# Weight preparation regrouped, three staging buffers in rotation and mixtures issued earlier, in a fused attention and two-layer MoE kernel

## The chip, the cores and the metric

The kernel runs on one core of a Trainium2 chip. The metric is the device time of one execution in microseconds, and a smaller number is better. The engines are named as the profile names them: PE (matrix multiply; PEld is its weight load), DVE (vector), ACT (scalar and activation functions), POOL (general purpose) and SP (here only the issuer of DMAs).

## The reference

```python
attn = softmax_causal(q @ k.T / 8) @ v        # 2 batches, 12 heads, 448 tokens, head size 64
x = attn as (896 tokens, 768)
h = x @ moe_w_in                              # 768 x 2048
g = where(h >= 1, h, where(h <= -1, 0, (h + 1)**2 / 4))
x = g @ moe_w_out                             # 2048 x 768
xn = x / sqrt(mean(x*x) + 1e-6) * rms_g
out = (silu(xn @ w_gate) * (xn @ w_val)) @ w_out2   # 768 x 1536 twice, 1536 x 768
```

The weights arrive as 64-bit floats.

## The kernel before

**Precision and weights.** Each operand of a matmul is split into a high and a low part in the PE's fp32r format, and a product is three matmuls per block of the contraction: high by high, high by low, low by high. A block of weights of 128 x 768 (an item) goes through steps that `w_run` issues one at a time between the matmuls, at a rate set by `w_pace` and `RATE` (four times the number is the steps per call), no further than `w_cap`; `w_need` issues whatever is still missing. A plain item has four steps (`plain_steps`): `w_low` (ACT scales the upper word, line 167, and POOL makes the lower bits from a byte, line 175), `w_sign` (empty for all but the first items), `w_high` (DVE joins both into an fp32 value, line 193) and `w_lo` (`parts`: ACT rounds the value to the high part, line 200, and POOL subtracts it, line 201). The items are loaded by DMAs of 768 KB into three staging buffers; the next load into a buffer is issued by `w_next` when its item has been used.

**Order of the work.** Attention first; then the two token halves go through w_in (line 370) and w_out (line 632, `out1`, half 0, then half 1); then the gate and value products (line 728, `product`, 9 matmuls of 448 columns each); then w_out2 (line 884, `out2`, half 0, then half 1). Every engine works off its queue in the order in which this Python issues the instructions.

**Second product.** Gate and value are computed by a scheme of seven products per block f of 128 hidden columns and both halves (Strassen with common sums), on sums of weights (`pair_steps`, blocks of 5 or 7 parts) and on mixtures T1 to T4 and B22 of the two normalised halves (`mix_a`, `mix_b`, made in PSUM and SBUF after `rms_sum` and `rms_spread` of half 1). The first NA = 4 blocks get two of the seven as `head(f)` and `tail(f)` from plain gate items, while the mixtures are made. A block's gate and value items were put through 1 + 6 steps into `rawg`, `rawv` and `sraw`; `sraw` lies in the third staging buffer, so that gate, value and all later items use two, and w_out2's items three. Block 0 is prepared during `out1`, block 1 between the mixtures and in iteration 0, each later one during the iteration before its own. The result of each product is taken over at once by DVE or ACT (`p1` to `p7`), and the weight steps come after that.

```python
for p, g, n in run:
    if g >= 0:
        p(g)                       # product and its take-over
    w_run(n if f < NF - 1 else 2)
```

**Last product.** `out2(0)` prepares one w_out2 item for each group of 18 matmuls (`w_pace(1)`, four steps) and splits one activation (`split2`, lines 867 and 868).

Of the kernel before, what the change touches and what calls it, by code (L numbers as in the profile page):

```python
# [16 lines left out]
ALU = mybir.AluOpType  # L17
# [24 lines left out]
def kernel(  # L42
# [387 lines left out]
    rawv = AF.at(TMO, NK * P)  # L430
    sraw = AF.at(STO + 2 * 2 * NK * P, 4, KP)

# [8 lines left out]
    def pair_steps(n, f):  # L441
        bl = block(f)
        g1, g2 = rawg[:, :KP], rawg[:, KP:]
        v1, s1, s2 = (bank(i)[:, :KP] for i in (5, 6, 7)) if f else (rawv[:, :KP], sraw[:, 2], sraw[:, 3])
        v2, s3, s4 = rawv[:, KP:], sraw[:, 0], sraw[:, 1]
        s12 = pst[:, 6:8, :KP] if f else sraw[:, 2:4]

        def tt(out, a, b, op):
            nc.vector.tensor_tensor(out=out, in0=a, in1=b, op=op)  # L449

        def gate_low():
            w_low(n)
# [12 lines left out]
        def sums_a():
            tt(s1, v1, v2, ALU.add)
            tt(s3, g1, v1, ALU.subtract)

        def sums_b():
            tt(s2, s1, g1, ALU.subtract)  # L470
            tt(s4, g2, s2, ALU.subtract)
            parts(bl[:, 0, 4], bl[:, 1, 4], v2)

        def parts_a():
            nc.scalar.copy(bl[:, 0, 0:2], s12)
            tt(bl[:, 1, 0:2], s12, b32(bl[:, 0, 0:2]), ALU.subtract)

        def parts_b():
            parts(bl[:, 0, 2:4], bl[:, 1, 2:4], sraw[:, 0:2])
            if f == NF - 1:  # L480
                w_load(n + 2)

        return [gate_low], [gate_high, val_high, sums_a, sums_b, parts_a, parts_b]

# [4 lines left out]

    def plain(src, dst, st, early):  # L490
        work.append(plain_steps(len(items)))
        items.append((src, dst, early, st))

    def pair(f):
        work.extend(pair_steps(len(items), f))
        items.append((w_gate[f], None, False, len(items) % 2))
        items.append((w_val[f], None, False, len(items) % 2))

    assert len(items) % 2 == 0 and NA % 2 == 0
    for f in range(NA):  # L500
        plain(w_gate[f], gslot(f), len(items) % 2, False)
    for f in range(NF):
        pair(f)
    W2_FIRST = len(items)
    for kk in range(NF):
        plain(w_out2[kk * P:(kk + 1) * P], AR.at(W2_AT[kk], 2, NK * P), (2, 0, 1)[kk % 3], kk > 0)
    for w in work:
        steps.extend(w)
        ends.append(len(steps))

    body = tc.manual_schedule()
# [69 lines left out]
    if True:  # L581
# [7 lines left out]
        def gsplit(h, kk):  # L589
            t = gj[ngj[0] % 2] if ngj[0] not in (NM - 2, NM - 1) else AR.at(XO + (ngj[0] % 2) * 2 * S, 2, S)  # L590
# [35 lines left out]
        def out1(h, after, finish):  # L626
# [34 lines left out]

        def squares(h):
            def f(dm, y):
                sq, acc = SQ[h][dm % 2], ACC[h]
                nc.scalar.activation(sq if dm else acc, y, ACTF.Square)
                nc.scalar.activation(XF[h][dm], y, ACTF.Copy, scale=gvec[:, dm:dm + 1])
                if dm and h == 0:
                    nc.gpsimd.tensor_tensor(out=acc, in0=acc, in1=sq, op=ALU.add)
                elif dm:
                    nc.vector.tensor_tensor(out=ysum if dm < NK - 1 else acc, in0=ysum if dm > 1 else acc, in1=sq,  # L670
                                            op=ALU.add)
            return f
# [79 lines left out]

        XA = [bank(i % 2)[:, :S] for i in range(HK)]
        XB = [bank(2 + i % 2)[:, :S] for i in range(HK)]
        t2 = ysum

        def sub(out, a, b):
            nc.vector.tensor_tensor(out=out, in0=a, in1=b, op=ALU.subtract)

        def mix_a(i):  # L760
            x0 = XF[0]
            normalise(1, i, XA[i])
            normalise(1, i + HK, XB[i])
            xt = XF[1][i]
            sub(xt, XA[i], x0[i])
            sub(t2, XB[i], xt)
            operand(T1, i, xt)
            operand(T2, i, t2, nc.vector)

        def mix_b(i):  # L770
            x0 = XF[0]
            sub(x0[i], t2, x0[i])
            sub(x0[i + HK], x0[i + HK], t2)
            operand(T3, i, x0[i])
            operand(B22, i, XB[i], nc.vector)
            operand(T4, i, x0[i + HK])

        w_need(2 * NM + NA + 2)
        w_cap[0] += 2
# [12 lines left out]
        mix_b(1)  # L792
        tail(2)
        w_run(1)
        mix_a(2)
        tail(3)
        mix_b(2)

        yb = [bank(f % 2) for f in range(NF)]
        zb = [bank(2 + f % 2) for f in range(NF)]  # L800
        cb = bank(4)

        def p1(f):
            product(yb[f], op(f, A11), B11)
            nc.scalar.copy(A[f][1], yb[f][:, :S])

        def p6(f):
            product(yb[f], op(f, S2), T2, first=f < NA)
            if f < NA:
                add(TMP[f][0], yb[f], A[f][1])  # L810
# [3 lines left out]
        def p7(f):  # L814
            product(zb[f], op(f, S3), T3)

        def p5(f):
            product(yb[f], op(f, S1), T1, first=False)
            if f < NA:
                add(TMP[f][1], yb[f], A[f][1])  # L820
                nc.scalar.activation(A[f][0], A[f][0], ACTF.Silu)
            else:
                nc.scalar.copy(TMP[f][1], yb[f][:, :S])
            add(TMP[f][1], zb[f], TMP[f][1])

        def p2(f):
            product(cb, op(f, A12), B21)
            add(A[f][0], cb, A[f][1])
            nc.scalar.activation(A[f][0], A[f][0], ACTF.Silu)

        def p4(f):
            z = zb[f][:, :S]
            product(zb[f], op(f, A22), T4, first=False)
            add(z, zb[f], TMP[f][0])
            mul(A[f][0], z, A[f][0])

        def p3(f):
            y = yb[f][:, :S]
            product(yb[f], op(f, S4), B22, first=False)
# [3 lines left out]
            mul(A[f][1], y, TMP[f][1])  # L843

        NP2 = 2 * NM + NA
        for f in range(NF):
            w_need(NP2 + 2 * f + 2)
            w_cap[0] = NP2 + 2 * f + 4 if f < NF - 1 else W2_FIRST + 4
            if f < NA:
                m = f < 2  # L850
                run = [(p4, f - 1, 2), (p6, f, 2), (p7, f, 1), (p5, f, int(m)), (p3, f - 1, 2 - m)]
            else:
                run = [(p1, f, 1), (p4, f - 1, 1), (p6, f, 1), (p3, f - 1, 1), (p7, f, 1), (p5, f, 1), (p2, f, 1)]
# [96 lines left out]
```

## Time and profile before

| what | us |
|---|---|
| runs of the kernel | 638.01, 639.08, 640.96 |
| median | 639.08 |
| profiled execution | 638.73 |
| its span, first to last instruction | 637.0 |
| PE busy in it | 592.3 (93%) |
| DVE, ACT, POOL busy | 320.8, 331.2, 273.9 |
| mean granted PE clock | 0.981 |

The profile is of one execution. Its own time is 1.73 us more than its span. PE is the busiest engine by far; what can be gained is PE's idle time and the time in which its clock was below full.

### The profile page before, as it was taken

The numbers are of one execution on the slowest core, as the hardware profiler recorded it, in microseconds if no ns is written. First come the engines' busy times: TensorE is split into PE (matmuls) and PEld (weight loads), VectorE is DVE, ScalarE is ACT, GpSimd is POOL, SyncE is SP. The second block draws the span as 40 slices with busy tenths as digits, with TensorE's granted clock in tenths as the row PEclk, the third lists the DMA queues.
The fourth block names the chain that finished last, engine by engine and source line by source line (L and its number), as shares of the span: only waits on it lengthen the run. The fifth ranks groups of instructions, "written<-read, shape, count | busy, mean of one in ns | idle before, by whom it ended". The sixth has DMA issues, their size and how long they took to land.

```text
span 637.0 us, 8655 instructions
## 1 busy us (share of the span) xinstructions
PE 592.3 (93%) x3236; PEld 510.5 (80%) x3236; DVE 320.8 (50%) x592; ACT 331.2 (52%) x648; POOL 273.9 (43%) x222
## 2 busy tenths in 40 slices
PE   6999999999999999999988888699999976979997
PEld 4666667999999899999977677599888865768997
DVE  5877871343233333412456877657677625553210
ACT  5888884466675734453435644355544535443212
POOL 3445432455655445441451643636655435661000
PEclk9999999999999999999999989899999978999999
DMA  8334311045444343210241124223333324421102
GB/s 292 98 128 138 118 50 50 7 158 182 151 155 170 120 149 109 90 50 6 94 145 55 50 82 166 100 99 100 118 133 140 106 100 148 150 99 46 42 1 86
DMA packets 17274, 68.19 MB, mean 107 GB/s; under 512 B 2064, under 2 KB 6672, under 8 KB 17232
## 3 DMA queue, kind: packets, MB, share of 16 engines
q1 hardware_dynamic: 17232, 67.64, 31.7%
q8 instruction: 25, 0.41, 0.3%
q14 instruction: 17, 0.14, 0.1%
HBM read 64.88 MB, written 2.75 MB: 106 GB/s over the span
## 4 chain that ended last, share of the span: by engine, by line
PE 61%; POOL 12%; DVE 11%; issue 10%; ACT 4%; DMA 2%; POOLq 0%; SPq 0%; ACTq 0%; DVEq 0%
PE ps L370 18%; PE ps L632 14%; PE ps L884 9%; POOL ar L201 6%; PE ps L276 5%; POOL af L175 5%; PE ps L728 5%; PE ps L307 4%; PE ps L355 4%; DVE af L193 3%; DVE af L449 2%; PE ps L341 2%; DVE ps L449 1%; DMA af<-in_w_out 1%; ACT ar L702 1%
## 5 line engine op out<-in xcount | busy, mean ns | idle before, releaser
L201 POOL TENSOR_TENSOR ar<-af,ar 128x768 fp32r<-128x768 f32 (+1 forms) x80 | 142.0, 1775 | 216.6 <-ACT ar L200 211.7
L728 PE MATMUL ps<-ar 128*128 128x448 f32 x756 | 167.8, 382 | 21.0 <-DVE af L738 5.3
L728 PEld LDWEIGHTS ps<-ar 128*128 128x128 f32 x756 | 146.8, 197 | 41.2 <-DVE af L738 7.8
L632 PE MATMUL ps<-ar 128*128 128x448 f32 x576 | 118.3, 366 | 2.4 <-ACT ar L592 2.0
L193 DVE SCALAR_TENSOR_TENSOR af<-af 128x768 int32<-128x768 int32 (+1 forms) x73 | 78.0, 1070 | 81.9 <-POOL af L175 81.7
L370 PE MATMUL ps<-ar 128*128 128x448 f32 x576 | 117.5, 366 | 0.0
L632 PEld LDWEIGHTS ps<-ar 128*128 128x128 f32 x576 | 107.9, 188 | 12.0 <-ACT ar L592 2.4
L370 PEld LDWEIGHTS ps<-ar 128*128 128x128 f32 x576 | 108.0, 188 | 8.6
L200 ACT CAST ar<-af 128x768 fp32r<-128x768 f32 (+1 forms) x80 | 65.6, 819 | 81.8 <-DVE af L193 81.7
L884 PE MATMUL ps<-ar 128*128 128x448 f32 x432 | 89.9, 368 | 10.0 <-DVE ar L868 8.4
L884 PEld LDWEIGHTS ps<-ar 128*128 128x128 f32 x432 | 80.5, 188 | 19.5 <-DVE ar L868 11.2
L175 POOL TENSOR_SCALAR af<-af 128x768 int32<-128x768 uint8 x72 | 73.4, 1019 | 14.4 <-DMA af<-in_w_out 5.1
L167 ACT ACTIVATE af<-af 128x768 f32<-128x768 f32 x66 | 58.6, 905 | 35.4 <-DMA af<-in_w_out 22.9
L593 DVE TENSOR_TENSOR ar<-af,ar 128x448 fp32r<-128x448 f32 x32 | 27.5, 864 | 67.4 <-ACT ar L592 67.4
L291 ACT ACTIVATE af<-ps,nm 112x336 f32<-112x336 f32 (+2 forms) x96 | 46.9, 501 | 7.6 <-DVE nm L283 7.6
L868 DVE TENSOR_TENSOR ar<-af,ar 128x448 fp32r<-128x448 f32 x24 | 27.0, 1140 | 45.9 <-ACT ar L867 45.9
L283 DVE CUSTOM_DVE_ANT_0 ps<-ps,af 112x336 f32<-112x336 f32 (+2 forms) x96 | 41.5, 474 | 13.0 <-PE ps L276 11.9
L276 PE MATMUL ps<-af 64*112 64x448 f32 (+3 forms) x192 | 35.5, 451 | 5.4 <-DVE af L254 5.3
L592 ACT CAST ar<-af 128x448 fp32r<-128x448 f32 x32 | 17.8, 565 | 34.9 <-PE ps L632 34.8
L383 DVE SCALAR_TENSOR_TENSOR af<-af,ps 128x448 f32<-128x448 f32 x32 | 19.3, 616 | 26.1 <-ACT af L379 26.1
L378 ACT ACTIVATE af<-ps,half 128x448 f32<-128x448 f32 x32 | 20.1, 629 | 20.8 <-PE ps L370 20.8
L307 PE MATMUL ps<-ident,af 112*112 112x112 f32 x240 | 30.6, 266 | 0.0
(79 smaller groups left out, 481.0 us busy)
## 6 DMA issues: line engine op xcount, KB each, us to landing
af<-in_w_out SPq DMA_DIRECT2D x28, 768.0 KB, 4.2
af<-in_w_in SPq DMA_DIRECT2D x16, 768.0 KB, 4.3
af<-in_w_gate SPq DMA_DIRECT2D x16, 768.0 KB, 4.3
af<-in_w_val SPq DMA_DIRECT2D x12, 768.0 KB, 4.3
af<-in_kT SPq DMA_DIRECT2D x12, 224.0 KB, 2.6
af<-in_qT SPq DMA_DIRECT2D x12, 224.0 KB, 3.5
af<-in_v SPq DMA_DIRECT2D x12, 224.0 KB, 2.5
out_T<-af SPq DMA_DIRECT2D x12, 224.0 KB, 1.9
```

Source lines behind the costliest of these rows:

```text
L167: nc.scalar.activation(c, c, ACTF.Prelu, scale=2.0 ** -112, alpha=-2.0 ** 32)
L175: nc.gpsimd.tensor_scalar(out=words(n, 0, I32), in0=b, scalar1=1.0 / 32, scalar2=-31.0 / 64, op0=ALU.mult, op1=ALU.add)
L193: nc.vector.scalar_tensor_tensor(out=out.bitcast(I32), in0=words(n, 1, I32)[:, c], scalar=3, in1=words(n, 0, I32)[:, c], op0=ALU.logical_s ...
L200: nc.scalar.copy(hi, src)
L201: nc.gpsimd.tensor_tensor(out=lo, in0=src, in1=b32(hi), op=ALU.subtract)
L276: nc.tensor.matmul(bs[j][:C, o:o + (c + 1) * C], lhsT=q[r, c * C:(c + 1) * C], rhs=k[r, :(c + 1) * C], start=True, stop=True, skip_group_c ...
L291: nc.scalar.activation(Pn[:C, j, poff[c]:poff[c] + w], sbank[n][j][:C, o:o + w], ACTF.Exp, bias=nm[:C, j, c:c + 1], scale=-1.0, accum_out= ...
L307: nc.tensor.transpose(bs[j][:C, o:o + C], Pn[:C, j, poff[c] + kc * C:poff[c] + (kc + 1) * C], ident[:C, :C])
L370: nc.tensor.matmul(out, lhsT=w[:, a, k * P:(k + 1) * P], rhs=x[:, c, k], start=(k == 0 and n == 0), stop=(k == NK - 1 and n == 2))
L632: nc.tensor.matmul(ybs[dm][:, :S], lhsT=w[:, a, dm * P:(dm + 1) * P], rhs=t[:, c], start=(n == 0 and i == 0), stop=(n == NM - 1 and i == 2))
L728: nc.tensor.matmul(b[:, :S], lhsT=w(a, k), rhs=x[:, c, k], start=first and k == 0 and i == 0, stop=(k == HK - 1 and i == 2), skip_group_ch ...
L884: nc.tensor.matmul(obs[dm][:, :S], lhsT=w[:, a, dm * P:(dm + 1) * P], rhs=t[:, c], start=(kk == 0 and i == 0), stop=(kk == NF - 1 and i == 2))
```

## The change

Weight steps are regrouped so that the instructions of one step do not wait for one another on another engine; the steps of a pair are six (`low`, `high`, `sums_a`, `sums_b`, `hi`, `lo`), both items together. The working space `sraw` leaves the staging buffer, and all items rotate over three. Blocks 0 and 1 of the second product are both prepared during `out1` of half 1, in SBUF (`pre`), and `RATE[5]` is 0.6 in place of 0.42; four more buffers serve the last splits there. In the loop over blocks, weight steps are issued between a product and its take-over. The mixtures keep three sets of PSUM banks, and the low halves of T1 and T2 and all of T4 and B22 are made later; `head(1)` moves ahead of `rms_sum(1)`; the last three scalings of half 1 are issued after its last square; a Silu on a small tile is issued after the Sqrt. `p3` of the block before moves ahead of `p7` in the first blocks. w_out2's items go through three steps (`low`, `high` into `rawg` or `rawv`, `parts`), those of three successive items interleaved, and `out2(0)` issues three steps per group.

```diff
-    RATE = (0.35, 0.35, 0.8, 0.2, 0.6, 0.42)
+    RATE = (0.35, 0.35, 0.8, 0.2, 0.6, 0.6)
...
     def pair_steps(n, f):
+        pre = f < 2
+        sr = AF.at(3 * S, 4, KP) if pre else AF.at((2 * NM - 4) * S, 2, KP)
+        v1, s1, s2 = (rawv[:, :KP], sr[:, 2], sr[:, 3]) if pre else (bank(i)[:, :KP] for i in (5, 6, 7))
...
-        return [gate_low], [gate_high, val_high, sums_a, sums_b, parts_a, parts_b]
+        def low():
+            w_low(n)
+            w_low(n + 1)
+        def high():
+            w_high(n, rawg)
+            w_next(n)
+            w_high(n + 1, v1, v2)
+            w_next(n + 1)
+        def sums_a():
+            if f >= NA:
+                parts(bl[:, 0, 5:7], bl[:, 1, 5:7], rawg.rearrange("p (a b) -> p a b", a=2))
+            parts(bl[:, 0, 4], bl[:, 1, 4], v2)
             tt(s1, v1, v2, ALU.add)
             tt(s3, g1, v1, ALU.subtract)
         def sums_b():
             tt(s2, s1, g1, ALU.subtract)
             tt(s4, g2, s2, ALU.subtract)
+        def hi():
+            nc.scalar.copy(bl[:, 0, 0:2], s12)
+            nc.scalar.copy(bl[:, 0, 2:4], sr[:, 0:2])
+        def lo():
             tt(bl[:, 1, 0:2], s12, b32(bl[:, 0, 0:2]), ALU.subtract)
+            nc.gpsimd.tensor_tensor(out=bl[:, 1, 2:4], in0=sr[:, 0:2], in1=b32(bl[:, 0, 2:4]), op=ALU.subtract)
+        return [], [low, high, sums_a, sums_b, hi, lo]
...
+    def w2_steps(n):
+        raw = (rawg, rawv)[n % 2]
+        dst = items[n][1]
+        def high():
+            w_high(n, raw)
+            w_next(n)
+        return [lambda: w_low(n), high, lambda: parts(dst[:, 0, :], dst[:, 1, :], raw)]
...
+    for i in range(NF + 2):
+        for j in range(3):
+            if 0 <= i - j < NF:
+                steps.append(w2[i - j][j])
...
+            elif ngj[0] > NM + 10:
+                t = AR.at(XO + 2 * NK * S + SLOT + (ngj[0] % 4) * 2 * S, 2, S)
...
-                    w_cap[0] = 2 * NM + min(NA + 2, max(0, n - 2))
+                    w_cap[0] = 2 * NM + min(NA + (2 if n < 12 else 4), max(0, n - 2))
...
             nc.scalar.activation(r, ms, ACTF.Sqrt)
+            if h:
+                nc.scalar.activation(t, ms, ACTF.Silu)
...
+        M1 = [bank(i)[:, :S] for i in (0, 1, 5)]
+        M2 = [bank(i)[:, :S] for i in (2, 3, 2)]
+        def mix(i):
+            x0, xb = XF[0][i], XF[1][i + HK]
+            normalise(1, i, M1[i])
+            normalise(1, i + HK)
+            sub(M1[i], M1[i], x0)
+            sub(M2[i], xb, M1[i])
+            sub(x0, M2[i], x0)
+            hi(T2, i, M2[i])
+            operand(T3, i, x0)
+            hi(T1, i, M1[i])
+        def mix_late(i):
+            x0 = XF[0][i + HK]
+            sub(x0, x0, M2[i])
+            operand(T4, i, x0)
+            operand(B22, i, XF[1][i + HK])
-        w_need(2 * NM + NA + 2)
+        w_need(2 * NM + NA + 4)
         head(0)
+        head(1)
         r1 = rms_sum(1)
-        head(1)
+        tail(0)
         rms_spread(1, r1)
-        mix_a(0)
-        tail(0)
-        mix_b(0)
+        mix(0)
         tail(1)
-        w_run(1)
         head(2)
-        mix_a(1)
+        mix(1)
         head(3)
-        mix_b(1)
+        lo(T2, 0, M2[0])
+        mix_late(0)
         tail(2)
-        w_run(1)
-        mix_a(2)
+        mix(2)
         tail(3)
-        mix_b(2)
+        lo(T2, 1, M2[1])
+        lo(T2, 2, M2[2])
-        yb = [bank(f % 2) for f in range(NF)]
-        zb = [bank(2 + f % 2) for f in range(NF)]
+        yb = [bank(f % 2 if f else 4) for f in range(NF)]
+        zb = [bank(2 + f % 2 if f else 6) for f in range(NF)]
...
             if f < NA:
-                m = f < 2
-                run = [(p4, f - 1, 2), (p6, f, 2), (p7, f, 1), (p5, f, int(m)), (p3, f - 1, 2 - m)]
+                run = [(4, f - 1, 1), (6, f, 1), (3, f - 1, 2), (7, f, 1), (5, f, 1)]
...
             for p, g, n in run:
                 if g >= 0:
-                    p(g)
+                    PRODUCT[p][0](g)
                 w_run(n if f < NF - 1 else 2)
+                if g >= 0:
+                    PRODUCT[p][1](g)
+                if f == 0 and p == 6:
+                    for i in range(HK):
+                        lo(T1, i, M1[i])
+                    mix_late(1)
+                    mix_late(2)
...
         p4(NF - 1)
-        w_run(2)
+        p4_post(NF - 1)
         split2(2)
         p3(NF - 1)
-        w_run(2)
+        p3_post(NF - 1)
...
-                    w_cap[0] = len(items)
-                    w_pace(1)
+                    w_run(3)
```

## Rows read from the trace of the kernel before

**Rows 1.** The page's span in 40 equal slices: PE's busy tenths and its granted clock.
```profile
PE   6999999999999999999988888699999976979997
...
PEclk9999999999999999999999989899999978999999
```

**Rows 2.** Groups by line, PE: busy us, mean ns, idle before and its releasers.
```profile
L728 PE MATMUL ps<-ar 128*128 128x448 f32 x756 | 167.8, 382 | 21.0 <-DVE af L738 5.3 <-DVE af L741 4.6 <-ACT af L812 4.0
...
L632 PE MATMUL ps<-ar 128*128 128x448 f32 x576 | 118.3, 366 | 2.4 <-ACT ar L592 2.0 <-DVE ar L593 0.2 <-DVE af L383 0.2
...
L884 PE MATMUL ps<-ar 128*128 128x448 f32 x432 | 89.9, 368 | 10.0 <-DVE ar L868 8.4 <-ACT ar L867 1.6
```

**Rows 3.** Timeline of PE, 312 to 640 us: start, us, instructions, idle before.
```profile
334.23 0.47 PE L632 MATMUL ps<-ar 128*128 128x448 f32 x1 [2.04 <-ACT ar L592]
334.89 6.75 PE L632 MATMUL ps<-ar 128*128 128x448 f32 x32 [0.19 <-DVE ar L593]
...
363.19 3.01 PE L728 MATMUL ps<-ar 128*128 128x448 f32 x9 [2.29 <-DVE af L758]
...
374.92 11.28 PE L728 MATMUL ps<-ar 128*128 128x448 f32 x54 [1.69 <-DVE af L738]
...
410.81 44.75 PE L728 MATMUL ps<-ar 128*128 128x448 f32 x207 [4.09 <-DVE af L741]
...
496.86 13.03 PE L728 MATMUL ps<-ar 128*128 128x448 f32 x63 [0.56 <-ACT af L805]
...
520.19 6.15 PE L728 MATMUL ps<-ar 128*128 128x448 f32 x18 [4.03 <-ACT af L812]
528.08 5.51 PE L728 MATMUL ps<-ar 128*128 128x448 f32 x18 [1.74 <-DVE af L738]
...
573.67 3.91 PE L884 MATMUL ps<-ar 128*128 128x448 f32 x18 [1.17 <-DVE ar L868]
578.76 54.79 PE L884 MATMUL ps<-ar 128*128 128x448 f32 x269 [1.17 <-DVE ar L868]
```

**Rows 4.** Windows: stretch, its length, busy of PE, PEld, DVE, ACT, POOL, then PEclk.
```profile
411.00:425.00 14.00, 14.00 (x59) 12.78 (x60) 7.16 (x13) 5.54 (x10) 6.46 (x5) 0.83 0.32 108
...
512.00:540.00 28.00, 19.13 (x72) 16.15 (x71) 11.21 (x13) 12.14 (x18) 12.11 (x9) 0.82 0.40 140
```

**Rows 5.** Timeline, all engines, 545 to 570 us, in out2(0).
```profile
566.19 1.86 POOL L201 TENSOR_TENSOR ar<-af,ar 128x768 fp32r<-128x768 f32 x1 [2.01 <-ACT ar L200]
566.61 1.93 DVE L868 TENSOR_TENSOR ar<-af,ar 128x448 fp32r<-128x448 f32 x1 [1.43 <-ACT ar L867]
...
569.32 0.96 DVE L193 SCALAR_TENSOR_TENSOR af<-af 128x768 int32<-128x768 int32 x1 [0.78 <-POOL af L175]
```

**Rows 6.** Groups by line, the other engines.
```profile
L175 POOL TENSOR_SCALAR af<-af 128x768 int32<-128x768 uint8 x72 | 73.4, 1019 | 14.4 <-DMA af<-in_w_out 5.1 <-DMA af<-in_w_val 3.6
...
L167 ACT ACTIVATE af<-af 128x768 f32<-128x768 f32 x66 | 58.6, 905 | 35.4 <-DMA af<-in_w_out 22.9 <-DMA af<-in_w_in 8.2 <-DMA af<-in_w_val 4.2
...
L703 POOL TENSOR_TENSOR ar<-af,ar 128x448 fp32r<-128x448 f32 x15 | 19.2, 1290 | 12.2 <-ACT ar L702 10.7 <-PE ps L728 1.3
...
L738 DVE TENSOR_TENSOR af<-ps,af 128x448 f32<-128x448 f32 x28 | 17.3, 618 | 4.3 <-ACT af L823 4.2
...
L449 DVE TENSOR_TENSOR ps<-ps,af 128x384 f32<-128x384 f32 x22 | 12.2, 556 | 0.1
```

**Rows 7.** Timeline, all engines: a table load near 373 us, and a wait for weights.
```profile
373.43 1.28 ACT L821 ACT_TABLE_LOAD   x1
374.73 0.58 ACT L821 ACTIVATE af<-af 128x448 f32<-128x448 f32 x1
...
516.87 1.71 ACT L167 ACTIVATE af<-af 128x768 f32<-128x768 f32 x2 [6.50 <-DMA af<-in_w_out]
516.94 0.86 POOL L175 TENSOR_SCALAR af<-af 128x768 int32<-128x768 uint8 x1 [5.09 <-DMA af<-in_w_out]
```

**Rows 8.** The page's DMA issues: median us from issue to landing.
```profile
af<-in_w_gate SPq DMA_DIRECT2D x16, 768.0 KB, 4.3
```

More of the change, by code (lines that the diff above doesn't have):

```diff
@@ L488, with plain @@
     work = [plain_steps(n) for n in range(len(items))]
-    def plain(src, dst, st, early):
-        work.append(plain_steps(len(items)))
+    def plain(src, dst, st, early, split=None):
         items.append((src, dst, early, st))
+        work.append((split or plain_steps)(len(items) - 1))
     def pair(f):
         work.extend(pair_steps(len(items), f))
-        items.append((w_gate[f], None, False, len(items) % 2))
-        items.append((w_val[f], None, False, len(items) % 2))
-    assert len(items) % 2 == 0 and NA % 2 == 0
+        items.append((w_gate[f], None, False, len(items) % NST))
+        items.append((w_val[f], None, False, len(items) % NST))
     for f in range(NA):
-        plain(w_gate[f], gslot(f), len(items) % 2, False)
+        plain(w_gate[f], gslot(f), len(items) % NST, True)
     for f in range(NF):
@@ L504 @@
     W2_FIRST = len(items)
+    def w2_steps(n):
[5 more added lines that the diff above has]
+        return [lambda: w_low(n), high, lambda: parts(dst[:, 0, :], dst[:, 1, :], raw)]
     for kk in range(NF):
-        plain(w_out2[kk * P:(kk + 1) * P], AR.at(W2_AT[kk], 2, NK * P), (2, 0, 1)[kk % 3], kk > 0)
-    for w in work:
+        plain(w_out2[kk * P:(kk + 1) * P], AR.at(W2_AT[kk], 2, NK * P), len(items) % NST, False, w2_steps)
+    for w in work[:W2_FIRST]:
         steps.extend(w)
         ends.append(len(steps))
+    w2 = work[W2_FIRST:]
+    for i in range(NF + 2):
+        for j in range(3):
+            if 0 <= i - j < NF:
+                steps.append(w2[i - j][j])
+                if j == 2:
+                    ends.append(len(steps))
     body = tc.manual_schedule()
@@ L589, in gsplit @@
         def gsplit(h, kk):
[L590 removed]
+            if ngj[0] in (NM - 2, NM - 1):
+                t = AR.at(XO + (ngj[0] % 2) * 2 * S, 2, S)
+            elif ngj[0] > NM + 10:
+                t = AR.at(XO + 2 * NK * S + SLOT + (ngj[0] % 4) * 2 * S, 2, S)
+            else:
+                t = gj[ngj[0] % 2]
             ngj[0] += 1
@@ L662, in squares, with scale @@
         def squares(h):
+            def scale(dm, y):
+                nc.scalar.activation(XF[h][dm], y, ACTF.Copy, scale=gvec[:, dm:dm + 1])
+            late = []
             def f(dm, y):
@@ L671, in f @@
                                             op=ALU.add)
+                late.append((dm, y))
+                if h == 0 or dm < HK or dm == NK - 1:
+                    for x in late:
+                        scale(*x)
+                    late.clear()
             return f
@@ L770, in mix_b, with hi, lo @@
[L770 to L776, printed above, removed]
-        w_need(2 * NM + NA + 2)
-        w_cap[0] += 2
+        def hi(dst, i, src):
+            nc.scalar.copy(dst[:, 0, i], src)
+        def lo(dst, i, src):
+            sub(dst[:, 1, i], src, b32(dst[:, 0, i]))
+        def mix(i):
[8 more added lines that the diff above has]
+            hi(T1, i, M1[i])
@@ L815, in p7, with p7_post, p5_post, p2_post @@
             product(zb[f], op(f, S3), T3)
+        def p7_post(f):
+            if f < NA:
+                add(TMP[f][1], zb[f], A[f][1])
+                nc.scalar.activation(A[f][0], A[f][0], ACTF.Silu)
+            else:
+                nc.scalar.copy(TMP[f][1], zb[f][:, :S])
         def p5(f):
             product(yb[f], op(f, S1), T1, first=False)
[L819 to L824, printed above, removed]
+        def p5_post(f):
+            add(TMP[f][1], yb[f], TMP[f][1])
         def p2(f):
             product(cb, op(f, A12), B21)
+        def p2_post(f):
             add(A[f][0], cb, A[f][1])
@@ L831, in p4, with p4_post @@
         def p4(f):
+            product(zb[f], op(f, A22), T4, first=False)
+        def p4_post(f):
             z = zb[f][:, :S]
-            product(zb[f], op(f, A22), T4, first=False)
             add(z, zb[f], TMP[f][0])
@@ L837, in p3, with p3_post @@
         def p3(f):
+            product(yb[f], op(f, S4), B22, first=False)
+        def p3_post(f):
             y = yb[f][:, :S]
-            product(yb[f], op(f, S4), B22, first=False)
             if f < NA:
@@ L843, in p3 @@
             mul(A[f][1], y, TMP[f][1])
+        PRODUCT = {1: (p1, p1_post), 2: (p2, p2_post), 3: (p3, p3_post), 4: (p4, p4_post), 5: (p5, p5_post),
+                   6: (p6, p6_post), 7: (p7, p7_post)}
         NP2 = 2 * NM + NA
```

37 lines of the change are left out of this document (6 added, 31 removed).

## The prediction

> **What bounds the kernel now.** I read the page's slices first: PE is at nine tenths or more from 16 us to about 318 us and only then shows holes [rows 1]. So I looked for PE's idle time behind that point alone. By line it is 21.0 us in the gate and value products, 2.4 us in `out1` and 10.0 us in `out2` [rows 2], 33.4 us in all. PE's timeline places it [rows 3]. Six places are seen there: a stop of 2.04 us in `out1`; several among the mixtures and the first four blocks, up to 4.09 us just ahead of 410.81; 0.56 us once in most of the later blocks (five such gaps); 4.03 and 1.74 us in the last block; and about 1.17 us per group in the second part of `out2(0)` (six such gaps).
>
> The second loss is the clock. From 411 to 425 PE never stood, yet the granted clock averaged 0.83; from 512 to 540 it averaged 0.82 [rows 4]. That is time at the lower of the two levels, 1.2 instead of 2.4 GHz: 18 matmuls take 6.15 and 5.51 us behind the stop of 4.03 us, where an undisturbed block takes 13.03 us for 63, 0.207 us each, or 3.72 us for 18 [rows 3]. Both stretches follow a stop of some 4 us, and 9 matmuls behind the stop of 2.29 us took 3.01 us.
>
> **The change part by part.** The sum is made against the profiled execution: 638.73 us, its span of 637.0 and 1.73 around it; the median of the runs lies 0.35 us higher. I split the end of the kernel at four landmarks of rows 3: the end of `out1` at 341.64 (334.89 + 6.75), the start of the first seven-product block at 410.81, the end of the second product at 533.59 (528.08 + 5.51) and PE's end at 633.55.
>
> *Half 1 of out1, end at 341.64 now.* Without the two stops in rows 3 it would be 339.4. The new pace is 2.4 steps per group against 1.68, and two pairs are prepared instead of one. What decides is one shared path: a DVE subtraction that reads two SBUF operands stretches to 1.93 us because it starts 0.42 us into a POOL instruction and ends 0.49 us after it [rows 5]. So I add DVE's two-operand work and POOL's work as if one engine did both. A pair in SBUF costs POOL two L175 (2 x 0.9 [rows 7]), a half-width and a full subtraction (1.0 + 1.86), and DVE one full and two half joins, four sums and a full subtraction (0.96 [rows 5] + 2 x 0.55 + 4 x 0.55 + 0.96, the half widths by L449 [rows 6]): 9.9 us. From group 10 to 14 there are two pairs, five splits at 0.6 and two mixed operands at 1.15: 25 us, in five groups of 18 x 0.204 = 3.67 us, 18.3 us. The backlog of some 6.5 us stands ahead of the last two splits, which are queued on DVE behind the pair's steps. The third staging buffer removes the wait for a DMA that was behind the old stop. Bounds: no stop at all (-2.2 us) and a stop of the whole backlog, with matmuls at the low clock behind it (+6). I take a stop of 3 us, under half of the backlog because the splits before still run ahead of PE, hence an end near 342.4: **+0.8 us**.
>
> *Mixtures and blocks 0 to 3, 69.2 us now (341.64 to 410.81).* I followed the new order with about 0.6 us for a DVE instruction (L738 has 0.618), 0.55 for an ACT copy (0.58 with a table [rows 7]), 1.15 for a POOL subtraction (1.29 in the mean with collisions [rows 6]; 1.86 x 448 / 768 is 1.09) and 1.86 for a product. Time runs from the end of `out1`. `head(0)` and `head(1)` cover the squares, so PE does not wait for the sum; `rms_sum` ends at 4.7. The Silu on the tile `t` adds a table load of 1.28 us [rows 7], and the next DVE instruction overwrites `t` and must wait for it: the factor is there at 7.6, `tail(0)` ends at 6.6, 1.0 us idle, `rms_spread` until 8.6. `tail(1)` and `head(2)` end at 12.4; `head(3)` needs the bank that `tail(1)`'s copy frees, and that copy is behind three mixture copies on ACT (13.6): 1.3 us idle. `head(3)`, `tail(2)`, `tail(3)` and block 0's `p6`, `p7`, `p5` then follow without a hole to 25.1, since no weight step is in the queues; now `p6(0)` starts 21.6 us behind `out1`, then 19.4. `p4(0)` waits for the last add on DVE (25.7) and, in its middle, for the third low half of T4 on POOL (28.5), and ends at 29.0. In rows 3 it is the first product behind 374.92 and ends 35.2 us behind `out1`: this part gives 6 us.
>
> Blocks 1 to 3 stay bound by DVE: seven take-over instructions at 0.62, joins of 0.96 + 2 x 0.56, four sums at 0.56 and a subtraction of 0.96, 9.6 us against 45 x 0.207 = 9.3 us of PE. Because the joins wait behind POOL's two L175, which wait behind POOL's last low half, DVE falls late: I get 13.1, 10.9 and 10.4 us, `p1(4)` at 60.2. That is 9.0 us less than 69.2. Bounds: 56 (DVE packed, its waits for POOL gone) and 62 (from `p4(0)` on no better than the 35.9 us from 374.92 to 410.81: 25.7 + 35.9). For PE stops of about 2 us in block 1 I add 1.5 us of lower clock, between 0 and 3.5. Sum: **-7.5 us**.
>
> The Trainium skill, ScalarE: Activation LUTs, section What ACT_TABLE_LOAD costs, gives 1.28 us and a drain of some 1.38 us for a switch of tables. Here the load is 1.28 us and the Silu starts 0.02 us behind it, so the trace shows no such drain; by the page the factor would be 1.4 us later and the sum below 1.4 us higher.
>
> *Blocks 4 to 11, 122.8 us now (410.81 to 533.59) for 522 matmuls.* At 0.207 they need 107.9. The 0.56 us per block is `p6` waiting for ACT's copy of `p1` behind a rounding that itself waits. Now two scalings at 0.9 stand ahead of that copy, behind the Silu of the block before: 0.75 + 0.58 + 1.7 + 0.55 = 3.6 us (an add with its start, a Silu, two scalings [rows 6, 7], a copy), against two products of 1.86, 3.7 us: it fits with little to spare (0.1 to 0.3 us, by how the instructions overlap). DVE has some 9.5 of 13.0 us. The stop of 4.03 us comes from an ACT queue in which the scaling waits 6.50 us for w_out2 [rows 7]; in rotation w_out2's first items load one block earlier and land in 4.3 us [rows 8]. With it goes the low clock, some 4 us. I leave 0.8 us; bounds 0 and 8 x 0.56 = 4.5. **-14.1 us.**
>
> *out2, 100.0 us now (533.59 to 633.55).* 432 matmuls at 54.79 / 269 = 0.204 need 88.0. A w_out2 item takes a period of 5.1 us today because each step waits for the one before on another engine; three items interleaved break that chain. The shared path remains: POOL 1.86 + 0.9, DVE 0.96 + 0.6, 4.3 us per item against 3.67 of PE. Two `w_run(2)` steps for each product of block 11 (14 steps) put three items ahead, 11 us, and nine more items lose 0.65 us each, 5.8 us, so PE doesn't run dry. At the start the splits stand on DVE behind `p4_post`, the joins and POOL: 1.7 us idle. I take 90.0, between 88.3 and 96: **-10.0 us.**
>
> Sum: +0.8 - 7.5 - 14.1 - 10.0 = -30.8, so 607.9. DVE instructions that do not depend on one another start closer together than the 0.6 us used; I take 1.4 us off for it: **606.5 us**.
>
> **The rivals.**
> *Preparation too early.* The full backlog of `out1` reaches PE, its last 33 matmuls and the heads run at the low clock, and block 1 stops long enough for it again: 5.2 us (6 in place of 0.8) and 4 us, with 3 us of the same collisions in `out2`: 606.5 + 12.2 = 618.7. For it speaks the collision, 1.93 us in place of 0.6 [rows 5]. Against it: the last splits have four buffers of their own and may run ahead. The Trainium skill, GPSIMD Engine Reference, section Specifications, says that POOL's SBUF interfaces are contended by DVE instructions with two SBUF inputs; the rows show it.
>
> *All covered.* Neither `out1` nor blocks 1 to 3 stop PE for over a microsecond: 606.5 - 3.0 (`out1` without a stop) - 2.8 (56 in place of 60.2, 1.4 of it counted) - 1.5 (no low clock) - 1.7 (`out2` without its first wait) = 597.5. For it: DVE is only some 0.3 us per block over PE. Against it: block 2 can't begin until iteration 1.
>
> *Slower.* In every later block ACT's two scalings now stand in front of the copy that frees `p6`. If each block's weights landed late, ACT would stand as it did for 6.50 us [rows 7], eight times: 606.5 + 8 x 6.2 (6.50 less the 0.3 to spare) = 656. It turns the result from 4.1 us lost per block on ((639 - 606.5) / 8), 4.4 us late. Against it: a load is issued some 9 us before its scaling and lands in 4.3 us [rows 8].
>
> *The gain is given back.* Most stops move instead of going: `out2` at DVE's and POOL's 4.3 us per item, block stops of 0.56 us left, blocks 1 to 3 as now: 606.5 + 6 + 3.7 + 1.8 + 2 (lower clock) + 5.2 = 625.
>
> **How the numbers follow.** Forecast (600 to 615) 0.58; preparation too early 0.16; all covered 0.11; given back 0.10; slower or equal 0.05. The range of 597 to 622 leaves out the slower case, most of the one that gives the gain back, and a little below. A run tells a change from none at about 0.5%, 3.2 us: faster 0.94, same 0.02, slower 0.04.
>
> **What would show it.** No gap of 0.56 us between blocks 4 to 11 and none at w_out2's start over 2 us; one run of `out2` matmuls at 0.204 without 1.17 us gaps; `p6(0)` some 19 to 20 us behind the end of `out1`; gaps of 1 to 2 us on DVE in blocks 1 to 3; splits late in the last groups of `out1`. Wrong would be: ACT's L167 waiting for DMA in each block, a clock below full for over 20 us behind 340, or L884 still released by L868 each group.

## The result, and the profile after

The changed kernel takes 612.62 us in the median (610.56 to 617.05) beside 640.02 for the kernel before, a ratio of 0.9585 (95% interval 0.9524 to 0.9646). In a second set of runs it was 0.9557 (0.9522 to 0.9591). The profiled execution took 610.56 us, its span 608.8; the forecast, made against a profiled execution, was 606.5. The profiled execution is the fastest of the four, so the forecast is 4.1 us too low against it and 6.1 us against the median.

PE's timeline of the changed kernel, 300 to 620 us (start, us, instructions, idle before). Line 650 is `out1`, line 757 the second product, line 937 `out2`.

```profile
301.38 22.35 PE L650 MATMUL ps<-ar 128*128 128x448 f32 x108
326.11 0.74 PE L650 MATMUL ps<-ar 128*128 128x448 f32 x1 [2.39 <-ACT ar L610]
327.34 10.87 PE L650 MATMUL ps<-ar 128*128 128x448 f32 x39 [0.48 <-DVE ar L611]
340.60 6.88 PE L650 MATMUL ps<-ar 128*128 128x448 f32 x32 [2.39 <-DVE ar L611]
...
354.49 1.15 PE L722 MATMUL ps<-ident,rr 112*128 112x112 f32 x8 [0.65 <-DVE rr L716]
...
360.64 11.21 PE L757 MATMUL ps<-ar 128*128 128x448 f32 x54 [1.35 <-ACT af L780]
372.11 1.69 PE L757 MATMUL ps<-ar 128*128 128x448 f32 x7 [0.26 <-DVE af L767]
375.09 7.96 PE L757 MATMUL ps<-ar 128*128 128x448 f32 x38 [1.29 <-POOL ar L732]
384.79 9.56 PE L757 MATMUL ps<-ar 128*128 128x448 f32 x45 [1.73 <-DVE af L767]
395.50 9.38 PE L757 MATMUL ps<-ar 128*128 128x448 f32 x45 [1.16 <-DVE af L767]
405.65 17.04 PE L757 MATMUL ps<-ar 128*128 128x448 f32 x81 [0.77 <-DVE af L770]
423.81 86.93 PE L757 MATMUL ps<-ar 128*128 128x448 f32 x423 [1.11 <-ACT af L838]
511.43 3.91 PE L757 MATMUL ps<-ar 128*128 128x448 f32 x18 [0.69 <-ACT af L857]
516.69 0.47 PE L937 MATMUL ps<-ar 128*128 128x448 f32 x1 [1.36 <-ACT ar L920]
517.43 87.94 PE L937 MATMUL ps<-ar 128*128 128x448 f32 x431 [0.26 <-DVE ar L921]
```

Set beside [rows 3]: the six gaps of about 1.17 us in `out2` and the 0.56 us per block are gone, the stops of 4 us have become 0.77 and 0.69, and two stops of 2.39 us stand in `out1` where there was one of 2.04. The same landmarks as in the prediction, taken from these rows:

| part, us | before | forecast | measured |
|---|---|---|---|
| end of `out1` | 341.64 | 342.4 | 347.48 |
| from there to `p1(4)` | 69.2 | 60.3 | 58.17 |
| `p1(4)` to the end of the second product | 122.8 | 108.7 | 109.69 |
| from there to PE's end | 100.0 | 90.0 | 90.03 |

The forecast column has the 1.4 us of closer DVE starts and the 1.5 us of lower clock in its second line. The end of `out1` is 340.60 + 6.88, `p1(4)` starts at 405.65 (81 + 423 + 18 = 522 matmuls follow in the second product), the second product ends at 511.43 + 3.91 = 515.34 and PE at 605.37. Three of the four lines came within 2.2 us, one 2.1 us below and one 1.0 us above the forecast; the first is 5.1 us off and makes the miss of 4.1 us, the others together giving 1.1 us of it back.

### The profile page after: what moved, and what is told of

The parts are those of the page before. It is cut to its first block, busy times and chain, and to the rows that moved or that the text cites. A ratio compares the mean times of both kernels' runs of the same rounds, so it can differ in the third digit from the quotient of the medians.

```text
span 608.8 us, 8661 instructions
## 1 busy us (share of the span) xinstructions
PE 583.8 (96%) x3236; PEld 507.2 (83%) x3236; DVE 306.1 (50%) x592; ACT 328.2 (54%) x649; POOL 274.6 (45%) x222
## 5 line engine op out<-in xcount | busy, mean ns | idle before, releaser
L201 POOL TENSOR_TENSOR ar<-af,ar 128x768 fp32r<-128x768 f32 (+1 forms) x68 | 119.3, 1760 | 151.4 <-ACT ar L200 135.1
L757 PE MATMUL ps<-ar 128*128 128x448 f32 x756 | 157.5, 368 | 8.4 <-DVE af L767 3.1
L650 PE MATMUL ps<-ar 128*128 128x448 f32 x576 | 121.9, 373 | 5.4 <-DVE ar L611 2.9
L193 DVE SCALAR_TENSOR_TENSOR af<-af 128x768 int32<-128x768 int32 (+1 forms) x74 | 73.0, 990 | 90.5 <-POOL af L175 64.9
L370 PE MATMUL ps<-ar 128*128 128x448 f32 x576 | 117.6, 366 | 0.0
L937 PE MATMUL ps<-ar 128*128 128x448 f32 x432 | 88.4, 366 | 1.7 <-ACT ar L920 1.4
L200 ACT CAST ar<-af 128x768 fp32r<-128x768 f32 (+1 forms) x68 | 55.1, 810 | 51.9 <-DVE af L193 47.4
L611 DVE TENSOR_TENSOR ar<-af,ar 128x448 fp32r<-128x448 f32 x32 | 27.4, 862 | 60.6 <-ACT ar L610 60.6
L921 DVE TENSOR_TENSOR ar<-af,ar 128x448 fp32r<-128x448 f32 x24 | 19.9, 844 | 34.8 <-ACT ar L920 34.8
L479 POOL TENSOR_TENSOR ar<-af,ar 128x768 fp32r<-128x768 f32 x12 | 22.4, 1865 | 33.0 <-ACT ar L475 33.0
```

Of the source, the lines that this page charges most:

```text
L193: nc.vector.scalar_tensor_tensor(out=out.bitcast(I32), in0=words(n, 1, I32)[:, c], scalar=3, in1=words(n, 0, I32)[:, c], op0=ALU.logical_s ...
L200: nc.scalar.copy(hi, src)
L201: nc.gpsimd.tensor_tensor(out=lo, in0=src, in1=b32(hi), op=ALU.subtract)
L370: nc.tensor.matmul(out, lhsT=w[:, a, k * P:(k + 1) * P], rhs=x[:, c, k], start=(k == 0 and n == 0), stop=(k == NK - 1 and n == 2))
L650: nc.tensor.matmul(ybs[dm][:, :S], lhsT=w[:, a, dm * P:(dm + 1) * P], rhs=t[:, c], start=(n == 0 and i == 0), stop=(n == NM - 1 and i == 2))
L757: nc.tensor.matmul(b[:, :S], lhsT=w(a, k), rhs=x[:, c, k], start=first and k == 0 and i == 0, stop=(k == HK - 1 and i == 2), skip_group_ch ...
```

## The experiments

All are made from the changed kernel; PE's timeline of a run is read at the same landmarks. Against the kernel before on the same chip, the medians give the ratios that are named.

**Order of the splits in `out1`.** The two stops of 2.39 us wait for splits (line 611 is DVE's half). Timeline of DVE in the changed kernel, just ahead of the last split:

```profile
337.12 2.89 DVE L450 TENSOR_TENSOR af<-af 128x384 f32<-128x384 f32 x4
...
339.93 0.62 DVE L611 TENSOR_TENSOR ar<-af,ar 128x448 fp32r<-128x448 f32 x1
```

The last split stands behind the four sums of pair 1. The first experiment moved splits ahead:

```diff
-                presplit(h * NM + n + 2)
+                if h and n >= 10:
+                    presplit(min(h * NM + n + 4, 31 if n < 13 else 32))
+                else:
+                    presplit(h * NM + n + 2)
```

> The changed kernel with the last splits of half 1 issued two groups earlier than now, so that they stand ahead of the pairs' weight steps in the queues of DVE and ACT; load unchanged. Theory (queue order): the changed kernel's three stops in the last groups of out1 (2.39, 0.48 and 2.39 us) come from splits queued behind the pairs' steps; they go, and with them the low clock behind them (39 matmuls in 10.87 us, where 0.204 us each would be 8.0), so out1 ends near 340 instead of 347.5 and the profiled execution takes 602 to 605 us against 610.56. Rival (load): DVE and POOL together have too much to do for these groups, whatever the order; the stops only move to the squares and the first heads, and the time stays within 2 us of 610.56.

It took 610.85 us, ratio 0.9514 (0.9472 to 0.9555). PE's timeline:

```profile
335.46 0.47 PE L650 MATMUL ps<-ar 128*128 128x448 f32 x1 [2.06 <-ACT ar L610]
339.37 8.70 PE L650 MATMUL ps<-ar 128*128 128x448 f32 x32 [3.43 <-DVE ar L611]
...
355.01 1.14 PE L725 MATMUL ps<-ident,rr 112*128 112x112 f32 x8 [0.64 <-DVE rr L719]
```

The stop at 326 went, but the last split, which still stood behind pair 1's joins, now stopped PE for 5.5 us at once. So this order did not separate the theories, though the time is the rival's. The next one gives the fifth split a buffer of its own and issues all five ahead of pair 1:

```diff
+                if h and n >= 10:
+                    presplit(30 if n == 10 else 32)
...
+            elif ngj[0] == 2 * NM - 1:
+                t = AR.at(SO, 2, S)
```

> The changed kernel with all five last splits of half 1 ahead of pair 1's weight steps (the fifth has a buffer of its own, so it needn't wait for PE); load unchanged. In the run with only some of them ahead PE stopped for 2.06 and 3.43 us, both times for the last split. Theory now (load): the work of two pairs on DVE, ACT and POOL ends near 343 to 345 us in any order; out1's stops go (its end near 340), but the squares stand behind the pair's steps on ACT, and PE waits for rms_sum by 4 to 6 us: 607 to 612 us. Rival (order of the queue): nothing takes the stops' place, 602 to 605 us.

610.01 us, ratio 0.9523 (0.9483 to 0.9563). PE's timeline:

```profile
304.07 36.98 PE L652 MATMUL ps<-ar 128*128 128x448 f32 x180
...
345.55 2.58 PE L762 MATMUL ps<-ar 128*128 128x448 f32 x9 [2.68 <-ACT af L687]
350.04 1.65 PE L709 MATMUL ps<-ones,af 128*112 128x1 f32 x8 [1.91 <-DVE af L697]
351.55 3.71 PE L762 MATMUL ps<-ar 128*128 128x448 f32 x9
355.05 1.88 PE L727 MATMUL ps<-ident,rr 112*128 112x112 f32 x8
```

`out1` now runs through without a stop, 180 matmuls, and ends near 341; PE then stands for 2.68 us behind a scaling on ACT and 1.91 us for the sum of the squares (lines 687 and 697 are `squares`), and `rms_spread`, the small matmuls with the factor, comes at 355.05, not before the 354.49 of the changed kernel. The stops came where the theory of load put them, 4.6 us in all. The clock has a part in this landmark, though. A window there (length, busy of PE, PEld, DVE, ACT and POOL, then the granted clock):

```profile
338.00:352.00 14.00, 9.41 (x43) 7.96 (x42) 9.31 (x14) 8.94 (x18) 4.69 (x3) 0.82 0.34 112
```

The small matmuls of `rms_sum` took 1.65 us in place of 0.85, and the 9 matmuls behind them 3.71 in place of 2.09, so that PE came to `rms_spread` 0.8 us after DVE had its factor ready (354.23). By an estimate from these times `rms_spread` would have come at some 353.5 us at the full clock, 1.0 us sooner than in the changed kernel; no run shows it.

**Pace.** `RATE[5]` back to 0.42, all else as changed.

> The changed kernel with the old pace in half 1 of out1 (0.42 in place of 0.6); all else as changed, so that most of pair 1's steps are issued behind the squares and ahead of the first heads. Theory (load): out1 ends near 341, but the pair's 10 to 12 us on DVE and POOL stand ahead of rms_sum's chain and of head(1)'s copy; PE waits there for 6 to 9 us: 611 to 617 us. Rival (the new pace alone is to blame): 603 to 607 us.

One run, 608.58 us. PE's timeline:

```profile
349.39 3.73 PE L757 MATMUL ps<-ar 128*128 128x448 f32 x9 [6.06 <-ACT af L776]
353.67 1.15 PE L722 MATMUL ps<-ident,rr 112*128 112x112 f32 x8 [0.55 <-DVE rr L716]
```

PE's largest stop here, 6.06 us, stands behind the heads and `rms_sum`, for a copy on ACT (line 776), as the theory said, and `rms_spread` came at 353.67. The time fell between the two expectations, but only 0.8 us of it was gained up to `rms_spread`; another 0.9 us is that 423 matmuls of the second product took 86.01 us in this execution and 86.93 in the other, without a hole in either.

**Less work, and an earlier start.** Leaving out the four sums of pair 1:

```diff
+            if f != 1:
                 tt(s1, v1, v2, ALU.add)
                 tt(s3, g1, v1, ALU.subtract)
...
+            if f != 1:
                 tt(s2, s1, g1, ALU.subtract)
                 tt(s4, g2, s2, ALU.subtract)
```

> The changed kernel without the four DVE sums of pair 1 (block 1 is multiplied with leftovers of block 0, so its output is not the reference's); they took 2.89 us. Theory (two pairs' work is a chain that must end before the mixtures): rms_spread comes at 351 to 352 us in place of 354.5, and the whole is 2.5 to 3.5 us shorter. Rival (order of the queue, or PE itself): rms_spread stays within 0.7 us of 354.5.

One run, 610.22 us; the second product ends at 513.59 in place of 515.34 (what follows, `out2`, took 1.4 us longer in this execution, which the last section shows to come and go). PE's timeline:

```profile
338.79 6.88 PE L652 MATMUL ps<-ar 128*128 128x448 f32 x32 [0.64 <-DVE ar L613]
...
352.68 1.14 PE L724 MATMUL ps<-ident,rr 112*128 112x112 f32 x8 [0.65 <-DVE rr L718]
```

The last stop falls from 2.39 to 0.64 us and `rms_spread` comes 1.8 us sooner: more than the rival's 0.7 us, less than the 2.5 us expected, as 2.89 us of DVE were taken out. Less work moved the landmark, by some 60% of what was taken out. The sums stood ahead of the last split on DVE, so this run by itself does not tell work from order; with it stands the run with five splits ahead, where the order alone did not bring the landmark forward. What is left of the stop lies at the split itself: it waited for ACT's half and took 1.08 us on DVE in place of 0.62, beside a POOL subtraction. An earlier start of the pairs, with the five splits ahead:

```diff
-    RATE = (0.35, 0.35, 0.8, 0.2, 0.6, 0.6)
+    RATE = (0.35, 0.35, 0.8, 0.2, 0.6, 0.7)
...
-(2 if n < 12 else 4)
+(2 if n < 11 else 4)
```

> Five splits ahead; the pairs' steps start some two groups earlier (2.8 steps per group, pair 1 from group 11); the work is unchanged. Theory (the chain of two pairs): begun near 309 in place of 317, it ends near 337 in place of 343; out1 ends near 340 without a stop over 1 us, rms_spread comes at 347 to 349 in place of 354.5, and the time is 603 to 606 us. Rival (collisions with the mixed operands that POOL makes in groups 6 to 11): the chain only gets longer, rms_spread at 353 to 356, 609 to 613 us.

611.36 us, ratio 0.9542 (0.9511 to 0.9573). PE's timeline:

```profile
326.26 0.47 PE L652 MATMUL ps<-ar 128*128 128x448 f32 x1 [4.23 <-ACT ar L612]
327.49 19.59 PE L652 MATMUL ps<-ar 128*128 128x448 f32 x89 [0.76 <-DVE ar L613]
...
354.01 1.14 PE L727 MATMUL ps<-ident,rr 112*128 112x112 f32 x8 [0.63 <-DVE rr L721]
```

The rival was right: PE stood for 4.23 us for an earlier split instead, and `rms_spread` came at 354.01. Pair 0's joins started only 1.7 us sooner (318.18 against 319.89): just ahead of them DVE stood 2.93 us for ACT's half of a split, which was queued on ACT behind two scalings (line 167) and a mixed operand's copy. A still earlier start:

> The same five splits ahead, and the pairs' steps begin earlier: 3.2 steps per group in place of 2.4, pair 1 allowed from group 10 in place of 12; work unchanged. Theory (load in too short a time): the two pairs are done by about 337 us, before the squares, out1 ends near 340 and rms_sum doesn't wait: 601 to 605 us. Rival (collisions): more of the pairs' work falls on the groups in which POOL makes mixed operands, the first splits come late instead, and PE stops for as long as before: 608 to 613 us.

619.27 us with a stop of 5.56 us. Here, by the addresses of the buffers, block 1's low parts are written over a split that group 10 has not yet used, which changes that product and its waits, so I draw nothing from its time.

**Three staging buffers.** Gate and value items in two buffers, as before the change:

```diff
-        items.append((w_gate[f], None, False, len(items) % NST))
-        items.append((w_val[f], None, False, len(items) % NST))
+        items.append((w_gate[f], None, False, len(items) % 2))
+        items.append((w_val[f], None, False, len(items) % 2))
```

> The changed kernel with gate and value items in two staging buffers as before, the third used for w_out2 alone. Theory (loads): w_out2's first items load late, ACT waits for a DMA again in block 11, PE stops for some 3 us there and runs at the low clock behind it: 616 to 619 us; in the blocks before, the next load is still in time. Rival (two buffers are enough): the stop at w_out2 came from the old order of steps alone, within 2 us of 610.56.

One run, 633.87 us, and not where the theory looked. PE's timeline, and ACT's waits for loads from 290 to 370 us (us in total, times, longest):

```profile
339.70 0.74 PE L652 MATMUL ps<-ar 128*128 128x448 f32 x1 [5.70 <-ACT ar L612]
...
537.10 0.47 PE L939 MATMUL ps<-ar 128*128 128x448 f32 x1 [1.34 <-ACT ar L922]
```

```profile
ACT af L167 <- DMA af<-in_w_gate: 12.6, 2, 6.3
```

Its `out1` ends at 368.99, 21.5 us later than in the changed kernel; 6.1 us of that are lost by `rms_spread` of half 0 (306.64 against 300.56). The two waits shown are for plain gate items, whose full-width roundings follow at 312.09 and 323.26: the issue of a load waits until POOL has split the item in its buffer. The value item of block 0 waits another 5.2 us for its load. The start of `out2` is as good as with three (1.34 us), so the theory falls. The third buffer carries the preparation in `out1`, and the stop of 4.03 us in block 11 [rows 3] was not a matter of the number of buffers.

**w_out2 in the old steps.** Plain items, four steps per group.

> The changed kernel with w_out2's items in the four old steps, one item after the other, four steps per group; all else as changed. Theory (chain): the interleaving is what removed the waits; the period of 5.1 us per item and the gaps of about 1.2 us per group come back in out2(0), 620 to 622 us. Rival (head start): the gain came from items that are ready before out2 begins, and the time stays under 614.

One run, 617.51 us. PE's timeline:

```profile
535.63 0.47 PE L930 MATMUL ps<-ar 128*128 128x448 f32 x1 [0.80 <-ACT ar L913]
536.29 3.72 PE L930 MATMUL ps<-ar 128*128 128x448 f32 x17 [0.19 <-DVE ar L914]
540.59 0.47 PE L930 MATMUL ps<-ar 128*128 128x448 f32 x1 [0.58 <-ACT ar L913]
```

The group period of about 5 us is back (535.63 to 540.59), and `out2` takes 99.1 us in place of 90.0. The period and the gaps are what the theory said; the sum is below 620 us because the second product ends 2.1 us sooner (513.20) and the start of `out2` waits 0.91 us in place of 1.62. But the chain of waits in this run also goes through a load:

```profile
540.02 4.26 DMA af<-in_w_out
```

A plain item issues the next load behind POOL's subtraction, the new steps issue it behind DVE's join (`w_next` in `high`). The run takes both back, so it does not separate the interleaving from the earlier loads.

**Place of the steps in the queue.** Take-over first, then the weight step:

```diff
-                w_run(n if f < NF - 1 else 2)
                 if g >= 0:
                     PRODUCT[p][1](g)
+                w_run(n if f < NF - 1 else 2)
```

> The changed kernel with each weight step issued behind the take-over of its product, as before the change. Theory (order in the queues): a gap of about 0.5 us per block of seven products comes back, and DVE in blocks 1 to 3 falls no later than now: 613 to 616 us. Rival (grouping alone): steps without waits between engines are short, so their place in the queue doesn't matter: within 1.5 us of 610.56.

613.22 us, ratio 0.9572 (0.9536 to 0.9607), no different from the changed kernel. PE's timeline:

```profile
405.63 107.73 PE L757 MATMUL ps<-ar 128*128 128x448 f32 x520 [0.46 <-POOL ar L201]
514.33 0.47 PE L937 MATMUL ps<-ar 128*128 128x448 f32 x1 [0.97 <-ACT ar L920]
518.73 89.63 PE L937 MATMUL ps<-ar 128*128 128x448 f32 x431 [3.93 <-DVE ar L921]
```

The median lies in the range of the theory, but that range was set against the profiled 610.56 us; the changed kernel's median is 612.62. PE's timeline decides, and the theory falls: no gap of 0.56 us comes back, 520 matmuls run without a hole, better than in the changed kernel, which has 1.11 and 0.69 us there. With two buffers those gaps did not come back either (423 matmuls without a hole), so of the place in the queue, the buffers and the grouping of the steps the last is left, which no run takes back by itself; the new order pays once, at the start of `out2` (1.36 + 0.26 us against 0.97 + 3.93).

**Two waits in the second product.** `p7` ahead of `p3` in the first blocks, and a tile of its own for the early Silu:

```diff
-                nc.scalar.activation(t, ms, ACTF.Silu)
+                warm = small.tile([P, NCH], F32, tag="warm", name="warm")
+                nc.scalar.activation(warm[:C], ms, ACTF.Silu)
...
-                run = [(4, f - 1, 1), (6, f, 1), (3, f - 1, 2), (7, f, 1), (5, f, 1)]
+                run = [(4, f - 1, 1), (6, f, 1), (7, f, 2), (3, f - 1, 1), (5, f, 1)]
```

> The changed kernel with p7 ahead of p3 in blocks 0 to 3, and with the early Silu writing a tile of its own, so that DVE needn't wait for it. Theory (DVE's order): the wait of 0.65 us for rms_spread goes; the add behind p7 no longer stands behind the Silu of p3, p4 of the next block starts on time, and blocks 1 to 3 take 9.6 to 10 us each in place of 10.7: 606 to 608 us. Rival (DVE's load): DVE is full anyway, the blocks stay at 10.5 us or more, 609 to 611 us.

One run, 610.28 us. PE's timeline:

```profile
355.11 1.04 PE L723 MATMUL ps<-ident,rr 112*128 112x112 f32 x8
...
386.56 9.55 PE L758 MATMUL ps<-ar 128*128 128x448 f32 x45 [0.50 <-DVE ar L450]
396.26 7.16 PE L758 MATMUL ps<-ar 128*128 128x448 f32 x34 [0.15 <-DVE ar L450]
405.11 104.42 PE L758 MATMUL ps<-ar 128*128 128x448 f32 x504 [1.68 <-DVE af L771]
```

The wait of 0.65 us is gone. From `p4(0)` (372.62, 372.11 in the changed kernel) to `p1(4)` it takes 32.5 us in place of 33.5, a microsecond over three blocks. By the starts of single matmuls the three stretches from `p4(0)` to `p4(1)`, `p4(2)` and `p1(4)` are 10.9, 10.1 and 11.4 us, in the changed kernel 12.7, 10.7 and 10.2: the waits of 1.73 and 1.16 us shrank to 0.50 and 0.15, and one of 1.68 us came at the end, for line 771, the take-over of `p3`, which now comes later and frees `p1(4)`'s bank. The time is the rival's. That DVE is full is not: it is busy 25.46 of these 32.5 us, and in each block it stands 0.96 us for ACT's Silu of `p3`.

**Together.** The five splits ahead, the earlier start and these two edits, with the changed kernel once more beside it on one chip.

> The changed kernel once more, beside the next three on one chip: 609 to 614 us, rms_spread of half 1 at 354.5 us, as in its first profile.

> The same, with the early Silu in a tile of its own and p7 ahead of p3 in blocks 0 to 3. From the run with these two alone (rms_spread 0.8 us sooner behind rms_sum, and about 1.5 us from there to the end of the second product): 600 to 604 us if the chain theory holds, 607 to 611 us if not.

The changed kernel again: 612.55 us (610.55 to 614.27), ratio 0.9557 (0.9522 to 0.9591). Together: 608.65 us (606.13 to 610.20), ratio 0.9486 (0.9444 to 0.9528). Every one of its four runs is below every one of the other's, so it is faster than the changed kernel too, by 3.9 us or 0.6% in the medians; the intervals of the ratios overlap at their ends. By its time the chain theory (600 to 604 us) does not hold. It keeps a stop in `out1` (4.24 us). In the profiles `rms_spread` comes 0.8 us sooner (353.38 against 354.18) and the second product ends 2.4 us sooner (511.65 against 514.10). These two profiled executions lie only 0.8 us apart, because `out2` took 92.9 us in one and 91.2 in the other; the rest of the 3.9 us is not located.

## Why the prediction was right, and where it was off

**Mixtures and blocks 0 to 3** went nearly step by step as written. `rms_spread` waited 0.65 us (1.0 forecast), `head(3)` 1.35 (1.3) for the copy behind the mixture's copies, `p4(0)` 0.26 and 1.29 (0.6 and some 1.4), the second on POOL's low half of T4; `p6(0)`, `p4(1)`, `p4(2)` and `p1(4)` came 18.7, 37.3, 48.0 and 58.2 us behind `out1` (19.4, 38.8, 49.7, 60.2). The lower clock that I added did not come: the granted clock was 1.00 from 347.5 to 405.6. That this 1.5 us and the 1.4 us taken off for closer DVE starts nearly cancel is luck. No run takes the new mixtures or the earlier block 1 back, so which of these moves gave the 11 us is not shown. The Silu's price is seen in the timeline of ACT and DVE:

```profile
352.35 1.28 ACT L712 ACT_TABLE_LOAD   x1
...
353.64 0.21 ACT L712 ACTIVATE rt<-ms 112x4 f32<-112x4 f32 x1
...
353.88 0.16 DVE L714 TENSOR_TENSOR rt<-rr 112x4 f32<-112x4 f32 x1 [1.34 <-ACT rt L712]
```

DVE waits 1.34 us to overwrite the tile, and the Silu starts 0.01 us behind its table. The drain of the Trainium skill (ScalarE: Activation LUTs, What ACT_TABLE_LOAD costs) doesn't show here either.

**Blocks 4 to 11** lost 1.8 us, 0.8 forecast. The 1.11 us is `p6` behind ACT's copy of `p1`, the place that I called just fitting; it is seen once, not in each block. The slower case, eight late loads, did not come: from 425 to 495 us ACT waited for no load.

**`out2`** took 90.03 us, 90.0 forecast, with 1.62 us at its start (1.7). The chain of waits shows the shared path of POOL and DVE as its period, 3.9 us (4.3 forecast):

```profile
529.91 2.09 POOL ar L201
...
533.81 2.09 POOL ar L201
```

That is over the 3.67 us of PE, and the items ready beforehand cover it, as worked out.

**Half 1 of `out1`** is the step that failed in size: "I take a stop of 3 us ... under half of the backlog because the splits before still run ahead of PE", +0.8 us. Measured were stops of 2.39 + 0.48 + 2.39 = 5.26 us, most of the backlog of 6.5 us, and behind the first of them the lower clock. A window of the changed kernel, with the columns as above:

```profile
327.34:338.21 10.87, 10.87 (x39) 9.33 (x39) 6.62 (x11) 5.67 (x9) 6.92 (x5) 0.74 0.22 71
```

Its 39 matmuls took 10.87 us where 0.204 each makes 8.0, another 2.9 us; less the stops of 2.2 us before, that is the +5.84 measured in place of +0.8, just inside the bound of +6. At the full clock the last stop would only have been longer, as the last split was ready at 340.55. The splits did not run far enough ahead: they are issued two groups before their use, and the one of the first stop stood on ACT (325.50) behind a mixed operand's copy that waited 1.08 us for DVE, busy until 324.47 with the joins and the first sums of block 0. That part of the rival "preparation too early" came true; its further 7 us did not.

What the experiments show is this. With the splits behind the pairs, ahead of them in part and in full, at the old pace and with an earlier start, `rms_spread` came at 354.5, 355.0, 355.1, 353.7 and 354.0 us while PE's stops moved; with less work it came at 352.7. No engine beside PE is full meanwhile. The changed kernel:

```profile
317.00:357.00 40.00, 34.09 (x156) 29.42 (x155) 22.18 (x36) 20.50 (x36) 16.95 (x12) 0.91 0.29 99
```

DVE is busy 22.18 of 40 us, ACT 20.50 and POOL 16.95. That the work of the pairs, the splits, the mixed operands and the squares on these three, with the waits between them, sets the time of this stage is supported, not proved. Whether the collisions, the chain of steps inside a pair or, with five splits ahead, the lower clock is the larger part was not separated.

## What to carry to other kernels

When every engine is fed from one queue in program order, moving helpers ahead can move the stall and not its sum, as it did here: find the landmark that hardly moves (here the small matmuls behind the squares, within 1.4 us in five orders) and try less work in front of it. Interleaving the steps of successive items, so that no step waits for the one just issued, paid together with the earlier loads (9 us in `out2`), and so did one buffer more, where the loads then come in time (21.5 us in `out1`). Adding the times of two engines that wait for one another as if one did both gave 4.3 us for a period of 3.9 and a backlog of 6.5 us for a delay of 5.26 + 2.9: take that backlog as the stop, unless room to run ahead has been counted out.

## What was not expected of the hardware

The lower clock behind a short stop comes in some executions and not in others. The start of `out2` is the same in four runs, a stop of 1.32 to 1.36 us and one of 0.26 or 0.27; the 431 matmuls behind it took 87.94 us in the changed kernel, 89.17 in the same kernel again, 89.33 without the four sums and 90.84 with all edits together, without a hole. Windows of 10 us there, for the first three:

```profile
517.00:527.00 10.00, 9.74 (x48) 8.89 (x48) 5.81 (x7) 6.66 (x12) 8.29 (x5) 1.00 0.48 157
```

```profile
516.00:526.00 10.00, 9.84 (x41) 9.00 (x42) 5.54 (x7) 6.75 (x11) 8.57 (x5) 0.83 0.48 158
```

```profile
516.00:526.00 10.00, 10.00 (x50) 9.10 (x49) 5.05 (x6) 6.63 (x10) 9.05 (x5) 1.00 0.46 152
```

The clock was 1.00 in the first and 0.83 in the second, 48 matmuls against 41. With all edits together it was 0.83 too. But the clock is not all: the third had 1.00 and still took 89.33 us. Windows of 70 us further on, for the same kernel again and for all edits together:

```profile
526.00:596.00 70.00, 70.00 (x347) 64.89 (x346) 22.22 (x25) 20.93 (x36) 19.47 (x11) 1.00 0.15 54
```

```profile
524.00:594.00 70.00, 70.00 (x340) 63.59 (x339) 22.24 (x25) 20.19 (x35) 19.06 (x11) 1.00 0.14 50
```

At a granted clock of 1.00 and with PE never idle, one execution ran 347 matmuls and the other 340, 2% fewer; without the four sums it was 341 in such a window. So an execution can lose 1 to 2 us here in either way, and the slowest lost in both. Why full-clock matmuls differ is open. It is part of why single runs here differ by 2 us.
